# A quarter of the products of E and v summed over two taps on VectorE in chunks 1 to 3, and one normalized tile transposed by DMA instead of TensorE

## The chip, the cores and the metric

The kernel runs on one core of a Trainium2 chip. The metric is the device time of one execution in microseconds (us). A profile of one execution gives the time of every instruction on TensorE (PE, with its weight loads as PEld), VectorE (DVE), ScalarE (ACT), GpSimd (POOL) and of the DMA queue that SyncE (SP) feeds.

## The reference: what is computed

The input x has 2048 rows of 512 numbers. It is normalized row by row, and the result feeds two branches: a local attention with 32 heads of 16 numbers, and a gated network with an inner width of 1792.

```python
xn = _layernorm(x, axis=-1)
s = _A_ref(xn, A_wqkv, A_wo)
g = _silu(_B_ref(xn, B_w_gate, B_w_up, B_w_down))
return x + s * g
```

In the attention every position looks at eight positions of its own head: itself and those 2, 4, ... 14 rows earlier. These eight are called taps here. The logits are products of q and k summed over 16 numbers; after the softmax, the weights of the eight taps multiply v, and the sum over the taps goes through wo:

```python
off = jnp.arange(W) * dil                      # W = 8, dil = 2
logits = jnp.einsum("bhsd,bhswd->bhsw", q, kg) * scale
attn = _softmax(logits, axis=-1)
o = jnp.einsum("bhsw,bhswd->bhsd", attn, vg)
```

The network is `_gelu(xn @ w_gate) * (xn @ w_up)` times w_down, then silu.

## The kernel before, in words

The rows are worked in NJ = 4 chunks of TQ = 512 columns (positions lie along the free dimension, features along the 128 partitions). For a chunk j the program is written out by hand in this order (L618 to L647): 14 `glu` steps (L437), each with four matmuls for the gate and four for the up projection, two ScalarE copies out of PSUM (gelu, and plain) and one VectorE product h; then 12 `qkv` steps of the next chunk (L295), whose PSUM results ScalarE copies to q, k and a staging tile for v; then four `down` steps (L450) of 14 matmuls each; then `divide` and four `finish` steps (L466), which multiply the attention with wo, combine both branches and store. All other work hangs on these steps through a table: `at(("glu", j, 3), ...)` (L487) has a function called just before that step. Each engine runs its instructions in the order in which they are emitted, so this table fixes what stands behind what.

The attention of a chunk goes as follows.

- `qk_products` (L320, VectorE) makes eight tiles q times shifted k. It is called during `qkv` of the same chunk (chunk 0: during `glu`).
- `logits` (L339, TensorE) sums them to eight taps times 32 heads, and ScalarE's exp writes E, with the low two bits of the tap (wl) and the head on the partitions, and the high bit (wh) and the position along the free dimension.
- v goes through DRAM (vT, L288 to L293) and is read back by `load_v` (L300) four times, each time shifted by two more positions, into the four groups of 32 partitions. So v_arr has tap wl and head on the partitions like E, and its 520 columns per feature let wh = 0 and wh = 1 be read as two windows, 8 columns apart.
- `av_product` (L399, VectorE) makes for four of the 16 features (a group g) and one wh the product of E and v in bfloat16: eight tiles per chunk. In chunks 1 to 3 they are called before `glu` steps 3 to 10 (L526, L527). For chunks 2 and 3 each is two instructions of 1024 columns, before that one of 2048.
- `sums(j)` (L508), called after the first `down` step (for the last chunk, before its `glu` step 12), has on TensorE the denominators, then `av_sums` (L412), and then the logits of the next chunk. Besides, it has the reciprocals on VectorE, a trip of these through DRAM (`rs_d`, `rb`), and `load_v` of the next chunk. `av_sums` sums the products over the four wl and both wh: 32 matmuls with 32 output columns each, four of them (i = 0 to 3) to four different groups of 32 PSUM partitions, wh = 0 starting and wh = 1 ending an accumulation.

Rows must also be normalized and transposed (xnT) ahead of their chunk. `moments` (L198) and `normalize` (L208) are VectorE work with one small GpSimd instruction; `transpose_by_dma` (L249) has the DMA write the transposed tile, `transpose` (L235) takes four TensorE transposes into PSUM and a ScalarE copy out of it. Tiles are of 128 rows. Tile 4, the first of chunk 1, is transposed by TensorE ahead of `glu` step 0 of chunk 0 (L609), tile 5 by DMA in two halves, one ahead of `load_v(0)` and one behind it (L610 to L612), tiles 6 and 7 whole by DMA behind that. For chunk 3, the `moments` run before `glu` steps 10 to 13 of chunk 1 and `normalize` before `qkv` steps 0 to 3 of chunk 2 (L498, L499).

Buffers that matter: PSUM tiles of `glu`, `qkv`, `down` and `finish` share four slots (`mm`, L74); ge and u have three slots each (`sm`, L67), h 14 (`hp`), the q tile one (`qp`, 4 KB per partition), the products share 12 (`prod`, L63), v_arr has one, shared with four of the tiles of q times k (tag "va").

Of the kernel before, what the change touches and what calls it, by code (L numbers as in the profile page):

```python
# [8 lines left out]
ALU = mybir.AluOpType  # L9
AF = mybir.ActivationFunctionType  # L10
BF16 = mybir.dt.bfloat16
F32 = mybir.dt.float32

P = 128
# [3 lines left out]
DIL = 2  # L18
WL = 4
WH = 2  # L20
PAD = 16
TQ = 512
# [6 lines left out]
def kernel(  # L29
# [13 lines left out]
    nc = tc.nc  # L43
    B, S, D = A_x.shape
    DF = B_w_gate.shape[1]
    NT, NC, NF, NJ = S // P, D // P, DF // P, S // TQ
    TPQ = TQ // P
# [5 lines left out]
    def pool(name, bufs, **kw):  # L53
        return ctx.enter_context(tc.tile_pool(name=name, bufs=bufs, **kw))
# [4 lines left out]
    qp = pool("qp", 1)  # L59
    kp = pool("kp", 2)  # L60
    ep = pool("ep", 1)
    vap = pool("vap", 1)
    prod = pool("prod", 12)  # L63
    hp = pool("hp", 14)
    xtp = pool("xtp", 2)
    op = pool("op", 1)
# [48 lines left out]
    def load_late_weights():  # L115
# [18 lines left out]
        out=vT.rearrange("(k p) n -> p k n", p=P)[:, :, 0:PAD],  # L134
# [134 lines left out]
    st = [dict(pk={}, pv={}, vst={}) for _ in range(NJ)]  # L269

    def copy_out(j, fo, ps, i0=0, n=TQ, m=1, copy=None):

        which, c = divmod(fo, NC)
        if which == 0:
            if "q" not in st[j]:
                st[j]["q"] = qp.tile([P, NC, TQ], BF16, name="q_sb")
            dst = st[j]["q"][:, c : c + m, i0 : i0 + n]
        elif which == 1:
            dst = k_sb[j][:, c : c + m, PAD + i0 : PAD + i0 + n]
        else:  # L280
            if c // 2 not in st[j]["vst"]:
                st[j]["vst"][c // 2] = vsp.tile([P, 2, TQ], BF16, name="vst")
            dst = st[j]["vst"][c // 2][:, c % 2 : c % 2 + m, i0 : i0 + n]
        if copy is None:
            nc.scalar.activation(out=dst, in_=ps, func=AF.Copy)  # L285
        else:
            copy(out=dst, in_=ps)
        if which == 2 and (c + m) % 2 == 0 and i0 + n == TQ:  # L288
            r, lo = slice((c // 2) * 2 * P, (c // 2 + 1) * 2 * P), PAD + j * TQ
            nc.sync.dma_start(  # L290
                out=vT[r, lo : lo + TQ].rearrange("(c p) n -> p c n", p=P),
                in_=st[j]["vst"][c // 2][:],
            )  # L293

    def qkv(j, fo):  # L295
        ps = mm.tile([P, 1, TQ], F32, name="qkv_ps", tag="mm")
        project(ps[:, 0, :], wqkv_sb, fo * P, j)
        copy_out(j, fo, ps[:])
# [40 lines left out]
    def logits(j):  # L339
        if j == 0:  # L340
            nc.scalar.preload_act_table(AF.Exp)
            quad = att.tile([P, NC, TQ], F32, name="L_ps", tag="quad")
            L = [quad[:, wh, :] for wh in range(WH)]
        else:
            L = [mm.tile([P, TQ], F32, name="L_ps", tag="mm")[:] for _ in range(WH)]
        E = st[j]["E"] = ep.tile([P, WH, TQ], BF16, name="E")
        for wh in range(WH):
            for c in range(NC):
                for wl in range(WL):
                    nc.tensor.matmul(  # L350
                        L[wh][H * wl : H * (wl + 1), :],
                        lhsT=dsum[:, c, :],
                        rhs=st[j]["pk"][WL * wh + wl][:, c, :],
                        start=(c == 0),
                        stop=(c == NC - 1),
                    )
        for wh in range(WH):
            nc.scalar.activation(out=E[:, wh, :], in_=L[wh], func=AF.Exp, scale=SCALE)
        if j == 0:
            for w in range(1, W):  # L360
                wh, wl = divmod(w, WL)
                nc.gpsimd.memset(E[H * wl : H * (wl + 1), wh, 0 : w * DIL], 0.0)

    def denominators(j):

        E = st[j]["E"]
        den = mm.tile([P, P], F32, name="den_ps", tag="mm")
        for wh in range(WH):
            for q in range(4):
                nc.tensor.matmul(  # L370
                    den[H * q : H * (q + 1), :],
                    lhsT=hsum[:],
                    rhs=E[:, wh, q * P : (q + 1) * P],
                    start=(wh == 0),
# [24 lines left out]
    def av_product(j, g, wh):  # L399
# [3 lines left out]
        for d in range(0, 4, n):  # L403
            nc.vector.tensor_tensor(  # L404
                out=pv[:, d : d + n, :],
                in0=st[j]["E"][:, wh, :].unsqueeze(1).to_broadcast([P, n, TQ]),
                in1=st[j]["va"][:, 4 * g + d : 4 * g + d + n, lo : lo + TQ],
                op=ALU.mult,
            )
        st[j]["pv"][g, wh] = pv  # L410

    def av_sums(j):  # L412

        o = att.tile([P, NC, TQ], F32, name="o_ps", tag="quad")
        for g in range(NC):
            for wh in range(WH):
                for i in range(4):
                    nc.tensor.matmul(  # L418
                        o[H * i : H * (i + 1), g, :],
                        lhsT=hsum[:],  # L420
                        rhs=st[j]["pv"][g, wh][:, i, :],
                        start=(wh == 0),
                        stop=(wh == WH - 1),
                    )
        st[j]["o"] = o

# [60 lines left out]
    def at(key, fn, *args):  # L487
        side.setdefault(key, []).append((fn, args))
# [5 lines left out]
    for i in range(TPQ):  # L494
        at(("down", 0, 1), moments, 2 * TPQ + i)
        at(("down", 0, 2), normalize, 2 * TPQ + i)
        at(("glu", 1, 0) if i else ("down", 0, 3), transpose_by_dma, 2 * TPQ + i)
        at(("glu", 1, 10 + i), moments, 3 * TPQ + i)  # L498
        at(("qkv", 2, i), normalize, 3 * TPQ + i)  # L499
        at(("glu", 2, 0) if i else ("down", 1, 3), transpose_by_dma, 3 * TPQ + i)  # L500

    for w in range(W):
        at(("glu", 0, w), qk_products, 0, [w], 0, NC)
    at(("glu", 0, 9), logits, 0)
    for i in range(8):
        at(("glu", 0, 9 + i) if i < 5 else ("qkv", 1, 0), av_product, 0, i // 2, i % 2)

    def sums(j):  # L508

        if j + 1 < NJ:  # L510
            nc.scalar.preload_act_table(AF.Exp)
        denominators(j)
        av_sums(j)
        if j + 1 < NJ:
            logits(j + 1)
        reciprocals(j)
        store_reciprocals(j)
        spread_reciprocals(j)
        if j + 1 < NJ:
            load_v(j + 1)  # L520

    for j in range(1, NJ):
        at(("qkv", j, 2), k_halo, j)
        for i in range(2):
            at(("qkv", j, 4 + 4 * i), qk_products, j, range(W), 2 * i, 2)
        for i in range(8):  # L526
            at(("glu", j, 3 + i), av_product, j, i // 2, i % 2)  # L527
    at(("glu", NJ - 1, 12), sums, NJ - 1)


# [6 lines left out]
    for _, ps in pairs:  # L537
        nc.tensor.matmul(
            ps, lhsT=zero[:], rhs=nc.const_aps.tensor(1.0, [P, 2, HQ], BF16),
            start=True, stop=False,  # L540
# [53 lines left out]
    for fo, ps in pairs:  # L594
        copy_out(0, fo, ps, 0, HQ, 2, nc.vector.tensor_copy if fo >= 8 else None)
# [5 lines left out]
    for n, fo in enumerate((0, 2, 4, 6, 8, 10)):  # L601
        ps = mm.tile([P, 2, HQ], F32, name="qkv_ps", tag="mm")

        w = HQ if n else P
        for i0 in range(0, HQ, w):
            for i in range(2):
                project(ps[:, i, i0 : i0 + w], wqkv_sb, (fo + i) * P, 0, HQ + i0, w)
        copy_out(0, fo, ps[:], HQ, HQ, 2)
    at(("glu", 0, 0), transpose, TPQ)  # L609
    at(("glu", 0, 0), transpose_by_dma, TPQ + 1, (0, 1))  # L610
    at(("glu", 0, 0), load_v, 0)
    at(("glu", 0, 0), transpose_by_dma, TPQ + 1, (2, 3))  # L612
    at(("glu", 0, 0), transpose_by_dma, TPQ + 2)
    at(("glu", 0, 0), transpose_by_dma, TPQ + 3)
    at(("glu", 0, 0), load_late_weights)
    for j in (2, 3):
        at(("glu", 0, 0), load_x, j * TPQ, TPQ)
# [58 lines left out]
```

## Time and profile before

| | us |
|---|---|
| time, median of 3 runs (lowest, highest) | 227.48 (227.48, 227.54) |
| span of the profiled execution | 225.6 |
| busy: TensorE | 220.3 |
| busy: VectorE | 151.9 |
| busy: ScalarE | 131.8 |
| busy: GpSimd | 22.0 |

The busy times show how full each engine is over the whole span. Which of them sets the end is read from the chain of waits: the profile follows the work that ended last backwards, step by step, to what released it. An engine that is not on that chain may be idle or busy without changing the time; how long it could be late is read from the time line of its instructions. One row of a time line is: start, length, engine, line, operation, output and inputs, shapes, count, and in brackets the idle time before it with what ended it.

### The profile page before, as it was taken

Reading aid. Unit: us, or ns where it says so; the run is one execution under the profiler, and the core shown is the slowest. Engines: PE = TensorE matmul, PEld = TensorE weight load, DVE = VectorE, ACT = ScalarE, POOL = GpSimd, SP = SyncE. Lnnn points to the kernel's source line nnn. Section 1 sums busy time; section 2 is a strip of 40 time slices with the busy share of each in tenths; the row PEclk is TensorE's granted clock in tenths of the full one; section 3 lists DMA queues with packets and bytes.
Section 4 is the critical chain, followed back from the end, with each engine's and each line's share of the span. In section 5 each row is a group of like instructions: output and inputs, shape, how many; then the busy total and the mean of one; then the engine's idle time right before and its main releaser. Section 6 shows DMA issues by size and latency. Waiting matters only on the chain.

```text
span 225.6 us, 3579 instructions
## 1 busy us (share of the span) xinstructions
PE 220.3 (98%) x1317; PEld 106.3 (47%) x1338; DVE 151.9 (67%) x281; ACT 131.8 (58%) x208; POOL 22.0 (10%) x67
## 2 busy tenths in 40 slices
PE   8999999999999999999999999999999999999994
PEld 4994444444444444444444444444444444444443
DVE  4688973999974499969804859924934358972352
ACT  4387779676721876767652466676763357655211
POOL 1026971000210000320000000000000000000000
PEclk9999999999999999999999999999999999999999
DMA  6998699952079910000219990000218940001002
GB/s 201 370 402 254 136 198 202 335 175 96 17 160 200 195 23 0 3 1 0 94 32 187 198 180 3 0 0 0 90 25 168 200 116 0 0 0 33 1 23 70
DMA packets 29746, 24.76 MB, mean 110 GB/s; under 512 B 10528, under 2 KB 29216, under 8 KB 29728
## 3 DMA queue, kind: packets, MB, share of 16 engines
q1 hardware_dynamic: 29728, 24.53, 45.1%
q8 instruction: 10, 0.16, 0.3%
q14 instruction: 8, 0.07, 0.1%
HBM read 18.74 MB, written 4.34 MB: 102 GB/s over the span
## 4 chain that ended last, share of the span: by engine, by line
PE 95%; ACT 1%; DVE 1%; DMA 1%; issue 1%; ACTq 0%
PE u_ps L261 22%; PE y_ps L455 21%; PE g_ps L261 20%; PE qkv_ps L261 16%; PE s_ps L471 6%; PE L_ps L350 3%; PE o_ps L418 3%; PE qk_ps L547 2%; ACT u L445 1%; DMA x_sb<-in_A_x_dram 1%; PE v_ps L547 1%; DVE stats L187 1%; PE den_ps L370 0%; PE tr L220 0%; PE trb L220 0%
## 5 line engine op out<-in xcount | busy, mean ns | idle before, releaser
L261 PE MATMUL u_ps<-xnT,wu_sb 128*128 128x512 bf16 x220 | 57.1, 379 | 0.4
L261 PE MATMUL g_ps<-xnT,wg_sb 128*128 128x512 bf16 x218 | 56.5, 379 | 0.2
L455 PE MATMUL y_ps<-wd_sb,h 128*128 128x512 bf16 (+2 forms) x233 | 49.3, 366 | 0.2
L445 ACT ACTIVATE u<-u_ps 128x512 bf16<-128x512 f32 x56 | 33.5, 598 | 16.9 <-PE u_ps L261 16.6
L443 ACT ACTIVATE ge<-g_ps 128x512 bf16<-128x512 f32 x56 | 33.5, 598 | 16.9 <-PE g_ps L261 15.9
L404 DVE TENSOR_TENSOR pv<-E,v_arr 128x1024 bf16<-128x1024 bf16 (+1 forms) x48 | 39.9, 863 | 3.7 <-DMA v_arr<-vT 3.7
L332 DVE TENSOR_TENSOR pk<-q_sb,k_sb 128x1024 bf16<-128x1024 bf16 (+1 forms) x56 | 39.0, 765 | 4.6 <-ACT k_sb L285 4.6
L447 DVE TENSOR_TENSOR h<-ge,u 128x512 bf16<-128x512 bf16 x56 | 23.8, 425 | 23.7 <-ACT u L445 22.1
L261 PE MATMUL qkv_ps<-xnT,wqkv_sb 128*128 128x512 bf16 (+2 forms) x197 | 36.8, 344 | 0.2
L455 PEld LDWEIGHTS <-h 128*128 128x128 bf16 x238 | 22.6, 98 | 26.5 <-issue 1.3
L261 PEld LDWEIGHTS <-wu_sb 128*128 128x128 bf16 x224 | 21.9, 98 | 26.5
L261 PEld LDWEIGHTS <-wg_sb 128*128 128x128 bf16 x224 | 21.7, 98 | 26.6 <-issue 0.8
L463 ACT ACTIVATE sl<-y_ps 128x512 bf16<-128x512 f32 (+2 forms) x17 | 9.7, 572 | 32.4 <-PE y_ps L455 28.9
L261 PEld LDWEIGHTS <-wqkv_sb 128*128 128x128 bf16 x200 | 18.9, 98 | 17.5
L479 DVE TENSOR_TENSOR m<-s_ps,sl 128x512 bf16<-128x512 f32 (+2 forms) x17 | 11.1, 655 | 19.7 <-PE s_ps L471 19.7
L430 DVE TENSOR_TENSOR oT<-o_ps,rb 128x1024 bf16<-128x1024 f32 x8 | 9.4, 1220 | 12.3 <-DMA rb<-rs_d 12.2
L204 POOL TENSOR_TENSOR rstd<-rstd,mhalf 128x1 f32<-128x1 f32 x12 | 8.0, 669 | 71.1 <-DVE rstd L201 71.1
L471 PE MATMUL s_ps<-wo_sb,oT 128*128 128x512 bf16 (+2 forms) x65 | 14.6, 366 | 0.2
L285 ACT ACTIVATE vst<-qkv_ps 128x512 bf16<-128x512 f32 x14 | 8.4, 597 | 3.7 <-PE qkv_ps L261 3.7
L285 ACT ACTIVATE k_sb<-qkv_ps 128x512 bf16<-128x512 f32 x14 | 8.4, 601 | 3.2 <-PE qkv_ps L261 3.2
L285 ACT ACTIVATE q_sb<-qkv_ps 128x512 bf16<-128x512 f32 x14 | 8.3, 603 | 3.0 <-PE qkv_ps L261 3.0
L471 PEld LDWEIGHTS <-oT 128*128 128x128 bf16 x68 | 6.5, 98 | 7.3
(64 smaller groups left out, 128.3 us busy)
## 6 DMA issues: line engine op xcount, KB each, us to landing
v_arr<-vT SPq DMA_DIRECT2D x16, 520.0 KB, 8.3
vT<-vst SPq DMA_DIRECT2D x8, 256.0 KB, 2.2
out_dram<-o_t SPq DMA_DIRECT2D x15, 128.0 KB, 3.4
wg_sb<-in_B_w_gate_dram SPq DMA_DIRECT2D x2, 896.0 KB, 10.2
wu_sb<-in_B_w_up_dram SPq DMA_DIRECT2D x2, 896.0 KB, 12.1
wd_sb<-in_B_w_down_dram SPq DMA_DIRECT2D x1, 1792.0 KB, 11.8
wqkv_sb<-in_A_wqkv_dram SPq DMA_DIRECT2D x4, 384.0 KB, 4.6
x_sb<-in_A_x_dram SPq DMA_DIRECT2D x3, 512.0 KB, 7.7
```

What stands on the lines that cost most here:

```text
L261: nc.tensor.matmul(ps, lhsT=w[:, dk, lo : lo + P], rhs=xnT[j][:, dk, i0 : i0 + n], start=(dk == 0), stop=(dk == NC - 1),)
L285: nc.scalar.activation(out=dst, in_=ps, func=AF.Copy)
L332: nc.vector.tensor_tensor(out=st[j]["pk"][w][:, c0 : c0 + n, :], in0=st[j]["q"][:, c0 : c0 + n, :], in1=k_sb[j][:, c0 : c0 + n, off : off ...
L404: nc.vector.tensor_tensor(out=pv[:, d : d + n, :], in0=st[j]["E"][:, wh, :].unsqueeze(1).to_broadcast([P, n, TQ]), in1=st[j]["va"][:, 4 * ...
L430: nc.vector.tensor_tensor(out=oT[:, g : g + 2, :], in0=st[j]["o"][:, g : g + 2, :], in1=st[j]["rb"][:].unsqueeze(1).to_broadcast([P, 2, TQ ...
L443: nc.scalar.activation(out=ge[:], in_=g_ps[:], func=AF.Gelu_apprx_tanh)
L445: nc.scalar.activation(out=u[:], in_=u_ps[:], func=AF.Copy)
L447: nc.vector.tensor_tensor(out=h[:], in0=ge[:], in1=u[:], op=ALU.mult)
L455: nc.tensor.matmul(y[:], lhsT=st[j][fc][:, tt * P : (tt + 1) * P], rhs=wd_sb[:, fc, cols], start=(fc == 0), stop=(fc == NF - 1),)
L463: nc.scalar.activation(out=sl[:], in_=y[:], func=AF.Silu)
L471: nc.tensor.matmul(s[:], lhsT=st[j]["oT"][:, g, tt * P : (tt + 1) * P], rhs=wo_sb[:, g, cols], start=(g == 0), stop=(g == NC - 1),)
L479: nc.vector.tensor_tensor(out=m[:], in0=s[:], in1=sl[:], op=ALU.mult)
```

## The change

There are three edits.

1. For group g = 0 (four of the 16 features) in chunks 1 to 3, a new function `av_pair` takes the place of two calls of `av_product`. For each of the four features it multiplies both halves of E with the two windows of v in one instruction, into a float32 tile `two` of 2 x 512 columns, and adds the two halves in a second instruction to one bfloat16 tile. The sum over wh is thus done by VectorE, and `av_sums` needs one pass of four matmuls for this group instead of two. The tile `two` takes the slot of q, whose last reader of that chunk is done by then. E is stored with wh reversed (`Eb`), so that its first half belongs to the window at column 0. The products of the other groups move from before `glu` steps 3 to 10 to before steps 1, 3, 5, 7, 9 and 10, and the pairs stand before steps 2, 4, 6 and 8.
2. `moments` and `normalize` of chunk 3 move from `glu` of chunk 1 and `qkv` of chunk 2 to the `down` steps of chunk 1, which leaves room on VectorE in `glu` of chunk 1.
3. Tile 4 is transposed by DMA, ahead of `load_v(0)`. Tile 5 is transposed whole behind it, and no half goes ahead.

Its aim is to take instructions from TensorE and give their work to VectorE and to the DMA.

```diff
-        E = st[j]["E"] = ep.tile([P, WH, TQ], BF16, name="E")
+        Eb = st[j]["Eb"] = ep.tile([P, WH, TQ], BF16, name="E")
+        E = st[j]["E"] = Eb[:, ::-1, :]
...
+    def av_pair(j, g, d):
+        if d == 0:
+            st[j]["pv"][g] = prod.tile([P, 4, TQ], BF16, name="pv", tag="prod")
+            st[j]["two"] = qp.tile([P, WH, TQ], F32, name="two", tag="q")
+        two = st[j]["two"]
+        v = st[j]["va"][:, 4 * g + d, 0:TQ]
+        nc.vector.tensor_tensor(
+            out=two[:],
+            in0=st[j]["Eb"][:],
+            in1=bass.AP(
+                tensor=v.tensor, offset=v.offset, ap=[v.ap[0], [WL * DIL, WH], [1, TQ]]
+            ),
+            op=ALU.mult,
+        )
+        nc.vector.tensor_tensor(
+            out=st[j]["pv"][g][:, d, :], in0=two[:, 0, :], in1=two[:, 1, :], op=ALU.add
+        )
...
         for g in range(NC):
-            for wh in range(WH):
+            pv = st[j]["pv"]
+            pvs = [pv[g]] if g in pv else [pv[g, wh] for wh in range(WH)]
+            for n, p in enumerate(pvs):
                 for i in range(4):
                     nc.tensor.matmul(
                         o[H * i : H * (i + 1), g, :],
                         lhsT=hsum[:],
-                        rhs=st[j]["pv"][g, wh][:, i, :],
-                        start=(wh == 0),
-                        stop=(wh == WH - 1),
+                        rhs=p[:, i, :],
+                        start=(n == 0),
+                        stop=(n == len(pvs) - 1),
                     )
...
-        at(("glu", 1, 10 + i), moments, 3 * TPQ + i)
-        at(("qkv", 2, i), normalize, 3 * TPQ + i)
+        at(("down", 1, 1), moments, 3 * TPQ + i)
+        at(("down", 1, 2), normalize, 3 * TPQ + i)
...
-        for i in range(8):
-            at(("glu", j, 3 + i), av_product, j, i // 2, i % 2)
+        for i in range(6):
+            at(("glu", j, 1 + i + min(i, 4)), av_product, j, 1 + i // 2, i % 2)
+        for d in range(4):
+            at(("glu", j, 2 + 2 * d), av_pair, j, 0, d)
...
-    at(("glu", 0, 0), transpose, TPQ)
-    at(("glu", 0, 0), transpose_by_dma, TPQ + 1, (0, 1))
+    at(("glu", 0, 0), transpose_by_dma, TPQ)
     at(("glu", 0, 0), load_v, 0)
-    at(("glu", 0, 0), transpose_by_dma, TPQ + 1, (2, 3))
-    at(("glu", 0, 0), transpose_by_dma, TPQ + 2)
-    at(("glu", 0, 0), transpose_by_dma, TPQ + 3)
+    for t in range(TPQ + 1, 2 * TPQ):
+        at(("glu", 0, 0), transpose_by_dma, t)
```

More of the change, by code (lines that the diff above doesn't have):

```diff
@@ L275, in copy_out @@
             if "q" not in st[j]:
-                st[j]["q"] = qp.tile([P, NC, TQ], BF16, name="q_sb")
+                st[j]["q"] = qp.tile([P, NC, TQ], BF16, name="q_sb", tag="q")
             dst = st[j]["q"][:, c : c + m, i0 : i0 + n]
```

## The prediction, made before the result was known

> **What bounds the kernel now.** I read the page's busy shares, then the chain of work that ended last in order of time, then VectorE's time line, and last the DMA share by stretches. The page:
>
> ```profile
> PE 220.3 (98%) x1317; PEld 106.3 (47%) x1338; DVE 151.9 (67%) x281; ACT 131.8 (58%) x208; POOL 22.0 (10%) x67
> ...
> PE 95%; ACT 1%; DVE 1%; DMA 1%; issue 1%; ACTq 0%
> ```
>
> TensorE carries the whole chain. The rest is the first load ahead of it and the last store. The chain in order of time (start, length, what):
>
> ```profile
> 11.67 5.27 PE qkv_ps L261 x56
> 16.94 0.22 PE tr L220 x4
> 17.17 0.21 PE g_ps L261
> ...
> 110.75 1.73 PE o_ps L418 x32
> ...
> 164.61 1.73 PE o_ps L418 x32
> ...
> 201.63 1.73 PE o_ps L418 x32
> 203.36 0.97 PE g_ps L261 x4
> ```
>
> The pieces join without a gap: the four transposes of tile 4 (L220) and the sums over the taps (L418) are on the path with their full length. Where the chain passes through ScalarE (0.61 us at 81.70, for one) TensorE isn't idle: from 80.74 to 83.33 three groups of 0.86 us fit exactly. So each matmul taken away shortens the end by what it streams, as long as no other engine becomes late. VectorE in chunk 3, before:
>
> ```profile
> 183.14 0.43 DVE L447 TENSOR_TENSOR h<-ge,u 128x512 bf16<-128x512 bf16 x1 [0.60 <-ACT u L445]
> 184.87 0.43 DVE L447 TENSOR_TENSOR h<-ge,u 128x512 bf16<-128x512 bf16 x1 [1.30 <-ACT u L445]
> 186.59 0.42 DVE L447 TENSOR_TENSOR h<-ge,u 128x512 bf16<-128x512 bf16 x1 [1.30 <-ACT u L445]
> 186.94 1.28 DVE L404 TENSOR_TENSOR pv<-E,v_arr 128x1024 bf16<-128x1024 bf16 x2
> 188.32 0.43 DVE L447 TENSOR_TENSOR h<-ge,u 128x512 bf16<-128x512 bf16 x1
> ...
> 199.02 1.29 DVE L404 TENSOR_TENSOR pv<-E,v_arr 128x1024 bf16<-128x1024 bf16 x2
> 200.41 0.43 DVE L447 TENSOR_TENSOR h<-ge,u 128x512 bf16<-128x512 bf16 x1
> ```
>
> h comes every 1.73 us, TensorE's step of eight matmuls; a pair of products just fills the time between. More VectorE work here makes h late. Prices, by shape:
>
> ```profile
> L404 DVE TENSOR_TENSOR pv<-E,v_arr 128x1024 bf16<-128x1024 bf16 x32 | 20.6, 685 | 0.0
> L404 DVE TENSOR_TENSOR pv<-E,v_arr 128x2048 bf16<-128x2048 bf16 x16 | 19.3, 1220 | 3.7 <-DMA v_arr<-vT 3.7
> L479 DVE TENSOR_TENSOR m<-s_ps,sl 128x512 bf16<-128x512 f32 x15 | 10.3, 686 | 18.3 <-PE s_ps L471 18.3
> L430 DVE TENSOR_TENSOR oT<-o_ps,rb 128x1024 bf16<-128x1024 f32 x8 | 9.4, 1220 | 12.3 <-DMA rb<-rs_d 12.2
> ```
>
> [...] 1024 elements cost 685 or 1220 ns.
>
> [...] The trace before has a float32 input (1220 ns) but no float32 product output. [...] 32 matmuls in 1.73 us is 0.054 each, while matmuls of full width take 0.86/4 = 0.216. [...]
>
> **The change part by part.**
>
> TensorE. Per chunk 1 to 3 four of 32 matmuls of `av_sums` go, one full set of four column groups: 4 x 0.054 = 0.216 us, in three chunks 0.65. The transposes of tile 4: 0.22. ScalarE's copy of that tile goes too (0.59 at 17.47), off the path. Weight loads go with their matmuls. Sum: 0.87 us.
>
> VectorE. A pair is one product with 2 x 512 float32 out and one sum of 512 from float32. I take the rows with a float32 operand: 1.22 and 0.69. Issued one behind another, independent instructions start sooner than their length says: 16 products of 1024 took 9.72 us, 0.61 each for 0.69; one of 2048 follows another instruction by 1.14 (37.52 to 38.66); h by 0.34. A dependent one starts 0.03 behind the end (m 178.21 + 0.69, o_t 178.93). So a pair takes 1.25 + 0.61 = 1.86. Two steps of `glu` now hold two h, one product (1.21, or 1.14 in chunk 1) and one pair: 0.68 + 1.21 + 1.86 = 3.75 against TensorE's 3.45. VectorE falls behind by 0.3 per pair, over four pairs 1.2.
>
> Walking chunk 3 in the clock of before: h(0) 183.14, product, h(1) 184.87, pair to 187.07, where h(2) was due at 186.59 (late 0.5); late by 0.8 at h(4), 1.1 at h(6), 1.4 at h(8), 1.0 at h(10); then it catches up 1.38 a step. The last product ends at 201.5 instead of 200.3. Its readers are the last four matmuls of `av_sums`, due at 201.63 + 24 x 0.054 = 202.93, and both clocks are shifted alike: 1.4 us in hand.
>
> In chunk 1 the walk gives at most 1.8 late. In chunk 2 products now begin behind h(0), about 129.2 - 0.4 us, but `load_v(2)`, last issued at about 119.6 and landing 11.3 later, lands near 130.9, less the 0.2 by which its release moves: VectorE waits some 1.5 us with h(1) behind it, and the walk gives at most 2.7 late. Chunk 1's v_arr lands at about 76.0, its first product is due 76.4; chunk 3's at 182.2, due 182.8, both about in time.
>
> How late may h be? h's queue holds ge and u. In chunk 1 ge of a step starts 1.55 ahead of its h (80.78, 82.33) and needs the h three steps back to have ended: 3 x 1.73 - 1.55 - 0.43 = 3.2 us late before ScalarE waits. Its PSUM slot is wanted by TensorE two steps on, 1.95 later than it is free now: 5.1 us before TensorE waits. 2.7 is well inside, so the VectorE work is costed at nothing.
>
> Moved `moments` and `normalize`: 4 x 1.01 + 1.38 = 5.4 us behind the reciprocals of chunk 1 (end 111.9), done by 117.3. VectorE waited there for rb until 119.05 (7.16 us), and the transpose of tile 12 is issued at 120.3. Nothing.
>
> The q slot: `two` needs q's readers done, VectorE itself; the next q copy by ScalarE waits for the last sum, some 5 us ahead. Nothing.
>
> DMA. Ahead of `load_v(0)` stands now a whole tile instead of a half (18.05). DMA shares (last but one column) by stretch:
>
> ```profile
> 21.00:22.00 1.00, 1.00 (x7) 0.42 (x5) 1.00 (x1) 0.73 (x2) 0.65 (x7) 1.00 0.27 50
> 22.00:23.00 1.00, 1.00 (x6) 0.46 (x5) 1.00 (x3) 0.71 (x2) 0.81 (x5) 1.00 0.04 12
> 23.00:24.00 1.00, 1.00 (x6) 0.47 (x5) 1.00 (x3) 0.60 (x1) 1.00 (x1) 1.00 0.00 0
> ```
>
> `load_v(0)` starts at 23.07, held by the landing of vT at 22.2, and the engines idle ahead of it. Three whole tiles at 75.23 to 79 took about 3.0 us of full share, so the extra half is some 0.5 us and fits. If not: v_arr(0) at 37.5 opens a VectorE stretch without a pause to 58.0, the last product of q and k. The logits read it at 58.62 - 0.22 + 27 x 0.054 = 59.86, 1.86 in hand. The half that moves behind `load_v(0)` delays xnT of chunk 1 by about 0.5: it landed by 29.7 + 8.9 = 38.6, wanted at 43.07. The weights for `glu` step 0 (5.59 + 11.0 = 16.6) are there in time too.
>
> **Unknown costs.** The float32 product: [...] I take 1.22. The extra half tile: 0.5 us by the share, at most half of its issue to landing, 5.4/2 = 2.7. The DMA round trip of the reciprocals of chunk 1 took 3.4 us (111.92 to 115.33), in others 1.5; twice the excess would bring 4.6 late, still inside 5.1.
>
> **The rivals.**
> - The float32 product runs at half rate. [...] Against it: the rows with float32 inputs[...]. 6%.
> - The whole tile ahead of `load_v(0)` costs 2.3 to 2.7 us there, and the logits of chunk 1 wait 0.4 to 0.8: 227.1, no change. Against it: the idle stretch above. 6%.
> - Waits that I costed at nothing take up part: h late beyond 3.2 in chunk 2 with small stalls of 0.2 to 0.3 us, or a bubble at a shorter set of sums: 226.85, still faster. 10%.
>
> **How the numbers follow.** 227.48 - 0.87 = 226.61. The likeliest case, 78%, ends within 0.2 of it. The range takes in the partial loss and the edge of the second rival, 226.35 to 227.1, and leaves out the first. Faster (below 227.03) 0.87, the same 0.06, slower 0.07.
>
> **What would show it.** Right: L418 with 116 matmuls, 1.51 us in chunks 1 to 3; no L220 piece at 16.9; `two` near 1.22 us; h at most 1.9 late in chunks 1 and 3 and 2.7 in chunk 2; TensorE's chain without gaps. Wrong: [...] a wait of the sums for pv near 201, ScalarE's ge waiting for h, or logits waiting for pk near 59.

## The result, and the profile after

The changed kernel takes 226.81 us (median of 6 runs, 226.36 to 227.06) against 227.48 us (median of 6 runs, 227.32 to 227.54). The ratio is 0.9969, 95% interval 0.9956 to 0.9982: 0.3% faster. The prediction was 226.6, within 226.35 to 227.1. The saving in the medians is 0.67 us, where 0.87 had been worked out; the section after the experiments takes up the missing 0.2 us.

From the page of the changed kernel, the engines' busy times and the shares of the chain that ended last:

```profile
PE 219.9 (98%) x1301; PEld 106.4 (47%) x1322; DVE 164.4 (73%) x295; ACT 131.4 (58%) x207; POOL 22.0 (10%) x67
...
PE 96%; ACT 1%; issue 1%; DVE 0%; ACTq 0%
```

VectorE has 12.5 us more work, TensorE 16 matmuls less, and the chain is still TensorE's. From the same chain in order of time (start, length, what):

```profile
12.02 5.27 PE qkv_ps L261 x56
17.29 0.22 PE g_ps L261
...
110.88 1.51 PE o_ps L442 x28
...
164.52 1.51 PE o_ps L442 x28
...
201.33 1.51 PE o_ps L442 x28
202.84 0.97 PE g_ps L261 x4
```

The four transposes that stood between the last qkv matmul and the first gate matmul are gone (16.94 to 17.17 before). The sums over the taps (now L442) have 28 matmuls in 1.51 us where there were 32 in 1.73, and the gate matmuls join them without a gap at 202.84. But the first line starts at 12.02 us, where before it started at 11.67, and nothing in the program ahead of it has changed.

From VectorE's time line in `glu` of chunk 3, its start and the rows around the last product, which stand in the order in which the program emits them (start, length, engine, line, operation, output and inputs, shapes, count, idle time before it):

```profile
182.84 0.42 DVE L471 TENSOR_TENSOR h<-ge,u 128x512 bf16<-128x512 bf16 x1 [0.60 <-ACT u L469]
183.18 1.28 DVE L406 TENSOR_TENSOR pv<-E,v_arr 128x1024 bf16<-128x1024 bf16 x2
184.56 0.42 DVE L471 TENSOR_TENSOR h<-ge,u 128x512 bf16<-128x512 bf16 x1
184.91 1.22 DVE L422 TENSOR_TENSOR two<-E,v_arr 128x1024 f32<-128x1024 bf16 x1
186.16 0.69 DVE L430 TENSOR_TENSOR pv<-two 128x512 bf16<-128x512 f32 x1
...
199.84 1.28 DVE L406 TENSOR_TENSOR pv<-E,v_arr 128x1024 bf16<-128x1024 bf16 x2
201.05 0.41 DVE L471 TENSOR_TENSOR h<-ge,u 128x512 bf16<-128x512 bf16 x1
```

VectorE has no idle time from 183.18 to the last product, but what it does is in time: the last product ends at 201.12 (199.84 + 1.28), while its readers, the last four matmuls of the sums, are due at 201.33 + 24 x 0.054 = 202.63. The prices of the two new instructions, from the groups by shape:

```profile
L422 DVE TENSOR_TENSOR two<-E,v_arr 128x1024 f32<-128x1024 bf16 x12 | 14.6, 1216 | 0.0
L430 DVE TENSOR_TENSOR pv<-two 128x512 bf16<-128x512 f32 x12 | 8.3, 692 | 0.4
```

### The profile page after: what moved, and what is told of

It is laid out like the page before. It is cut to its first block, busy times and chain, and to the rows that moved or that the text cites. A ratio compares the mean times of both kernels' runs of the same rounds, so it can differ in the third digit from the quotient of the medians.

```text
span 225.1 us, 3562 instructions
## 1 busy us (share of the span) xinstructions
PE 219.9 (98%) x1301; PEld 106.4 (47%) x1322; DVE 164.4 (73%) x295; ACT 131.4 (58%) x207; POOL 22.0 (10%) x67
## 4 chain that ended last, share of the span: by engine, by line
PE 96%; ACT 1%; issue 1%; DVE 0%; ACTq 0%
PE u_ps L261 22%; PE y_ps L479 21%; PE g_ps L261 20%; PE qkv_ps L261 16%; PE s_ps L495 6%; PE L_ps L352 3%; PE o_ps L442 3%; PE qk_ps L574 2%; ACT u L469 1%; PE v_ps L574 1%; PE warm_ps L244 1%; PE qk_ps L565 1%; PE den_ps L372 0%; PE v_ps L565 0%; PE trb L220 0%
## 5 line engine op out<-in xcount | busy, mean ns | idle before, releaser
L406 DVE TENSOR_TENSOR pv<-E,v_arr 128x1024 bf16<-128x1024 bf16 (+1 forms) x38 | 32.3, 880 | 1.9 <-ACT E L360 1.9
L204 POOL TENSOR_TENSOR rstd<-rstd,mhalf 128x1 f32<-128x1 f32 x12 | 7.0, 582 | 90.1 <-DVE rstd L201 90.1
L454 DVE TENSOR_TENSOR oT<-o_ps,rb 128x1024 bf16<-128x1024 f32 x8 | 9.4, 1219 | 7.7 <-PE y_ps L479 6.0
L422 DVE TENSOR_TENSOR two<-E,v_arr 128x1024 f32<-128x1024 bf16 x12 | 14.6, 1216 | 0.0
```

The source lines that it names most:

```text
L406: nc.vector.tensor_tensor(out=pv[:, d : d + n, :], in0=st[j]["E"][:, wh, :].unsqueeze(1).to_broadcast([P, n, TQ]), in1=st[j]["va"][:, 4 * ...
L422: nc.vector.tensor_tensor(out=two[:], in0=st[j]["Eb"][:], in1=bass.AP(tensor=v.tensor, offset=v.offset, ap=[v.ap[0], [WL * DIL, WH], [1, T ...
```

## The experiments

For every kernel I also read from the chain how long the program runs from the start of the 56 qkv matmuls, behind all that was seen to vary in the first 12 us, to the start of the last sum on VectorE. I call this the body. Starts and bodies are from one profile each. Each ratio compares with runs of the kernel before that stood beside that kernel; their medians lie between 227.48 and 227.54.

| kernel | time, median us | ratio to before (95%) | start of body | body |
|---|---|---|---|---|
| before | 227.48 | | 11.67 | 211.28 |
| the changed kernel | 226.81 | 0.9969 (0.9956 to 0.9982) | 12.02 | 210.41 |
| e1_tile4 | 227.25 | 0.9986 (0.9975 to 0.9997) | 11.82 | 211.06 |
| e2_pairs | 226.82 | 0.9969 (0.9956 to 0.9981) | 11.72 | 210.64 |
| e3_again | 226.68 | 0.9962 (0.9949 to 0.9974) | 11.89 | 210.41 |
| e6_two_tiles | 226.66 | 0.9961 (0.9948 to 0.9975) | 11.84 | 210.41 |
| e4_twice12 | 230.24 | 1.0117 (1.0102 to 1.0132) | 11.87 | 214.12 |
| e5_twice3 | 230.77 | 1.0138 (1.0123 to 1.0153) | 11.73 | 214.20 |
| e7_bf16_all | 224.74 | 0.9878 (0.9864 to 0.9893) | 12.26 | 208.46 |
| e9_bf16_all_again | 224.63 | 0.9871 (0.9854 to 0.9889) | 11.84 | 208.47 |
| e8_bf16_c0 | 224.99 | 0.9893 (0.9876 to 0.9909) | 12.12 | 208.25 |
| e10_bf16_c0_again | 224.76 | 0.9881 (0.9863 to 0.9900) | 11.62 | 208.38 |

### Each part alone, and the whole once more

The transposes alone (on the kernel before):

```diff
-    at(("glu", 0, 0), transpose, TPQ)
-    at(("glu", 0, 0), transpose_by_dma, TPQ + 1, (0, 1))
+    at(("glu", 0, 0), transpose_by_dma, TPQ)
     at(("glu", 0, 0), load_v, 0)
-    at(("glu", 0, 0), transpose_by_dma, TPQ + 1, (2, 3))
-    at(("glu", 0, 0), transpose_by_dma, TPQ + 2)
-    at(("glu", 0, 0), transpose_by_dma, TPQ + 3)
+    for t in range(TPQ + 1, 2 * TPQ):
+        at(("glu", 0, 0), transpose_by_dma, t)
```

> The kernel before with the third edit alone: tile 4 transposed whole by DMA ahead of the load of v for chunk 0, tile 5 whole behind it. Theory (each matmul taken from TensorE shortens the end by what it streams): 0.22 us less, 227.26, and from the start of the 56 qkv matmuls to the end of the span 0.22 less than before. Rival (the parts pay less than they stream, and the missing 0.2 us of the whole change is lost in one of them): less than 0.1 us here, if it is this part. If only the time ahead of the first transposes differs, the rival has no ground.

The pairs are the changed kernel with this edit taken back. That leaves edits 1 and 2 together; edit 2, the moved normalization, was not run by itself:

> The changed kernel with the transposes of tiles 4 and 5 as before (edits 1 and 2 alone). Theory: 0.65 us less than before, 226.83; o_ps 1.51 us in chunks 1 to 3. Rival: the pairs pay only some 0.45, because VectorE is late somewhere; then TensorE must show a gap in a glu stage or ahead of the sums.

And the changed kernel without any edit:

> The changed kernel once more, unaltered, to see how its time and its first 6 us vary. Theory: the sum of the two parts, 0.87 us, whenever the first transposed tile starts at 4.9 us as in the profile of before; up to 0.35 less[...], so 226.4 to 227.0. Rival: the saving is 0.67 us in every run, with the start at 4.9 as well.

The bodies are 0.22 us (211.28 to 211.06) and 0.64 us (to 210.64) shorter for the parts, and 0.87 us (to 210.41) for the whole, in both profiles of it. The parts add up to a hundredth. No part pays less than it streams, so the rival theory falls. The medians, 0.26, 0.69 and 0.83 us below the 227.51 of the runs of before that stood beside them, say the same more roughly. One part of my expectation for the third run was wrong: it started its first transposed tile at 4.83 us, as early as the kernel before, and yet its body started at 11.89. So the speed of TensorE's first matmuls isn't all that moves the start; more on that below.

### Two tiles ahead of the load of v

```diff
     at(("glu", 0, 0), transpose_by_dma, TPQ)
+    at(("glu", 0, 0), transpose_by_dma, TPQ + 1)
     at(("glu", 0, 0), load_v, 0)
-    for t in range(TPQ + 1, 2 * TPQ):
+    for t in range(TPQ + 2, 2 * TPQ):
         at(("glu", 0, 0), transpose_by_dma, t)
```

> The changed kernel with tile 5 also transposed ahead of the load of v for chunk 0, so that two whole tiles stand ahead of it instead of one. Theory (1.9 us in hand at the logits of chunk 1): v lands 0.5 to 1.5 us later than in the changed kernel, VectorE starts its products later by as much, and the time is the same within 0.1 us. Rival (a tile ahead of the load costs 2.3 us or more): the logits of chunk 1 wait near 59 us and the time grows by 0.4 us or more.

The time is the same (226.66 us) and the body too. v is there at 37.82 us, where the profiles with one tile ahead have 37.43 (e3_again) and 37.91 (e1_tile4), and before, with half a tile, 37.52. The second tile thus delays v by less than these differ (0.48 us), not by the 0.5 to 1.5 us that I expected. That fits the idle time of the DMA engines: in the changed kernel, with one whole tile ahead, the stretches (PE, PEld, DVE, ACT, POOL busy, granted clock, DMA share, GB/s) still have the hole, two microseconds at a share of 0.05:

```profile
22.00:24.00 2.00, 2.00 (x11) 0.88 (x9) 2.00 (x4) 1.44 (x3) 1.69 (x7) 1.00 0.05 8
```

The rival of a dear transfer ahead of the load falls.

### How much later VectorE may be: the slack by itself

The slack is how late VectorE may be before TensorE waits. To find it, the float32 product of each pair is issued twice, in chunks 1 and 2, or in chunk 3 alone (with `j == 3` for `j < 3`):

```diff
-        nc.vector.tensor_tensor(
-            out=two[:],
...
+        for _ in range(2 if j < 3 else 1):
+            nc.vector.tensor_tensor(
+                out=two[:],
...
```

> The changed kernel with the float32 product of each pair issued twice in chunks 1 and 2 (the same output twice, so the result is the same), 1.14 us more VectorE work per pair. Theory (TensorE waits once h is 5.1 us late): h(8) is late by 1.8 + 4.6 = 6.3 us in chunk 1 and 1.3 + 4.6 = 5.9 in chunk 2 if nothing waits; TensorE waits 1.2 and 0.8 us, so 2.0 us slower than the changed kernel, 228.8. Rival 1 (the slack is only the 3.2 us after which ScalarE waits): 3.1 + 2.7 = 5.8 us slower, 232.6. Rival 2 (VectorE in glu isn't tied to TensorE at all): no change.

> The changed kernel with the float32 product of each pair issued twice in chunk 3 alone. Theory: the last product of E and v ends at 201.1 + 4.6 = 205.7 us, TensorE's last four matmuls of the sums want it at 202.6, so TensorE waits 3.1 us there (part of it perhaps earlier, in glu) and the time is 229.9. Rival (the deadline at the sums isn't binding, only h is): 0.8 us slower, 227.6.

With more work in chunks 1 and 2 the body is 3.71 us longer than the changed kernel's (214.12 against 210.41). That lies between my 2.0 and the 5.8 of rival 1; rival 2, no change, falls. The time lines of that kernel in chunk 1, ScalarE's and then TensorE's, show where the loss is:

```profile
86.68 0.60 ACT L468 ACTIVATE ge<-g_ps 128x512 bf16<-128x512 f32 x1 [0.95 <-DVE h L472]
...
91.61 0.60 ACT L468 ACTIVATE ge<-g_ps 128x512 bf16<-128x512 f32 x1 [2.37 <-DVE h L472]
```

```profile
92.25 1.02 PE L261 MATMUL g_ps<-xnT,wg_sb 128*128 128x512 bf16 x4 [0.31 <-ACT ge L468]
...
97.18 1.02 PE L261 MATMUL g_ps<-xnT,wg_sb 128*128 128x512 bf16 x4 [1.32 <-ACT ge L468]
```

ScalarE's ge waits for h, and the gate matmuls wait for ge: the mechanism is the one that the prediction named. ScalarE waits first at 86.68, for an h(4) that is 3.9 us late (86.17 against 82.30), and TensorE loses nothing by it; so rival 1 falls as well. TensorE's first wait comes at 92.25. From 72.95 (first gate matmul) to 99.07 (first qkv matmul) this kernel takes 26.12 us, the changed kernel 24.17 (73.10 to 97.27): 1.95 us lost in chunk 1, and 1.76 in chunk 2.

Both sizes of the expectation were off. First, the second product, with the same output as the first, starts 0.02 us behind its end, so one more costs 1.27 us (78.11 to 80.63 for both and the dependence, against 1.25 for one), not 1.14. Second, the threshold for TensorE comes out of its two waits. h(6), behind the third pair, is 5.33 us late (91.09 against 85.76), and TensorE loses 0.47; h(8) is 6.81 late (96.02 against 89.21), less the 0.47 already lost, and TensorE loses 1.48. Both give 4.86 us, where the prediction had 5.1. The same two waits in chunk 2 give 4.85 and 4.83. About half of the difference lies in hand-overs between engines that the prediction left out: in the chain of this kernel 0.08 us pass from the end of h to ge (96.45 to 96.53) and 0.04 from ge to the gate matmuls (97.14 to 97.18). With 1.27 and 4.86 the expectation would have been 1.8 + 5.1 - 4.86 = 2.0 in chunk 1 (1.95 measured) and 1.3 + 5.1 - 4.86 = 1.5 in chunk 2 (1.76; there v landed only at 131.67, and VectorE waited 0.35 us for it).

In chunk 3 the loss is 3.79 us (214.20), where I expected 3.1; the rival with 0.8 falls. TensorE's time line of that kernel:

```profile
202.86 1.33 PE L443 MATMUL o_ps<-pv,hsum 128*32 128x512 bf16 x19 [1.61 <-DVE pv L431]
...
205.34 0.39 PE L443 MATMUL o_ps<-pv,hsum 128*32 128x512 bf16 x2 [0.54 <-DVE pv L406]
205.94 0.39 PE L443 MATMUL o_ps<-pv,hsum 128*32 128x512 bf16 x2 [0.21 <-DVE pv L406]
```

First the sums wait for the last pair, whose group is first in their order, and then for each later product. TensorE has no wait ahead of the sums here, so in chunk 3 their deadline is the tighter one. Four times 1.27 in place of 1.14 explains 0.5 of the 0.7 us. The rest is the end of the sums: the last two matmuls start behind the last product and take 0.39 us (205.94 to 206.33), where I had counted 0.054 each, as in an unbroken row. In the changed kernel the next gate matmuls start 1.72 us behind the last product (201.12 to 202.84), here 0.44 (205.89 to 206.33). So the slack at the sums is 1.3 us, and not the 1.5 between the last product and its due time.

### More from the same idea: bfloat16, two features at once, all groups

The experiments say that TensorE's saving comes in full as long as VectorE keeps within its slack. The float32 tile costs VectorE 1.86 us per feature (184.91 to the next h at 186.77). If the two products of a pair stay in bfloat16, as they did before the change, two features should fit in the same time: before, 2048 products in bfloat16 took 1220 ns and 1024 took 685. The sum of the two is rounded to bfloat16 as in the changed kernel. So all four groups of chunks 1 to 3 can be summed on VectorE:

```diff
-            st[j]["two"] = qp.tile([P, WH, TQ], F32, name="two", tag="q")
+        if "two" not in st[j]:
+            st[j]["two"] = qp.tile([P, 2, WH, TQ], BF16, name="two", tag="q")
...
-            in0=st[j]["Eb"][:],
+            in0=st[j]["Eb"][:].unsqueeze(1).to_broadcast([P, 2, WH, TQ]),
             in1=bass.AP(
-                tensor=v.tensor, offset=v.offset, ap=[v.ap[0], [WL * DIL, WH], [1, TQ]]
+                tensor=v.tensor, offset=v.offset,
+                ap=[v.ap[0], [VW, 2], [WL * DIL, WH], [1, TQ]],
...
-            out=st[j]["pv"][g][:, d, :], in0=two[:, 0, :], in1=two[:, 1, :], op=ALU.add
+            out=st[j]["pv"][g][:, d : d + 2, :],
+            in0=two[:, :, 0, :], in1=two[:, :, 1, :], op=ALU.add,
...
+        for i, fc in enumerate((1, 2, 3, 5, 6, 7, 9, 10)):
+            at(("glu", j, fc), av_pair, j, i // 2, 2 * (i % 2))
```

> All four groups of chunks 1 to 3 in pairs, with the products kept in bfloat16 and two features per instruction: a product of 2 x 2 x 512 and a sum of 2 x 512, eight of each per chunk. VectorE: 1.25 + 0.61 = 1.86 us for two features, 14.9 per chunk, about as much as the changed kernel's 14.7. Theory: TensorE loses 16 of 32 matmuls of the sums in three chunks, 3 x 0.86 = 2.59, and the transposes, 0.22: 224.67, and h is late by no more than 1.5 us. [...]

It takes 224.74 us, ratio 0.9878 (0.9864 to 0.9893), and once more 224.63, 0.9871 (0.9854 to 0.9889): faster than both kernels. In its trace h is late by up to 2.3 us in chunk 1 (90.21 against 87.87) and 2.0 in chunk 2, where I had expected no more than 1.5, and TensorE waits for it nowhere. The body is 2.82 us shorter than before, where 12 x 4 matmuls and the transposes give 2.81. From its groups by shape and its chain:

```profile
L422 DVE TENSOR_TENSOR two<-E,v_arr 128x2048 bf16<-128x2048 bf16 x24 | 29.3, 1219 | 0.5 <-DMA v_arr<-vT 0.5
...
L431 DVE TENSOR_TENSOR pv<-two 128x1024 bf16<-128x1024 bf16 x24 | 16.6, 692 | 0.8
```

```profile
111.11 0.86 PE o_ps L444 x16
```

2048 products in bfloat16 take as long as 1024 into float32 (1219 and 1216 ns), and 1024 bfloat16 sums as long as 512 of float32 (692 both). Before, without the overlapping windows of v, 2048 products in bfloat16 took 1220 ns, so the windows cost nothing that shows.

Last, the first group of chunk 0 in pairs too:

```diff
     for i in range(8):
-        at(("glu", 0, 9 + i) if i < 5 else ("qkv", 1, 0), av_product, 0, i // 2, i % 2)
+        if i < 2:
+            at(("glu", 0, 9 + i), av_pair, 0, 0, 2 * i)
+        else:
+            at(("glu", 0, 9 + i) if i < 5 else ("qkv", 1, 0), av_product, 0, i // 2, i % 2)
```

> As the kernel with all groups of chunks 1 to 3 in bfloat16 pairs, and also the first group of chunk 0. Theory: four matmuls less, 0.22 us, 224.45; VectorE has 1.4 us more work between the landing of v and the logits of chunk 1, whose last products of q and k end by 59.0 to 59.5 against a due time of about 60.0. Rival (the slack there is smaller): the logits of chunk 1 wait, and the gain is lost, 224.7 or more.

Both kernels were run side by side once more:

> The kernel with all groups of chunks 1 to 3 in bfloat16 pairs once more, beside the one that also has the first group of chunk 0 in pairs. Theory: 224.4 to 225.1, and 208.46 us from the start of the 56 qkv matmuls to the start of the last sum, as in its first profile; whatever differs lies in the first 12 us.

> The kernel that also has the first group of chunk 0 in pairs once more. Theory: 0.21 us less from the start of the 56 qkv matmuls to the start of the last sum (208.25), and the median 0.2 us under the other's, if the first 12 us fall alike. Rival: it is slower in time as its first four runs were (224.99 against 224.74), so something in chunk 0 waits in most runs, and its profile shows a gap of TensorE near 40 or 59 us.

The first profile has the 0.21 us in the body (208.25), the second only 0.09 (208.38). In its chain the logits of chunk 1 take longer than the 1.73 us that they stream:

```profile
58.13 1.86 PE L_ps L352 x32
```

Their last operand is there at 59.34 (49.63 + 9.71), 0.25 us ahead of 27 x 0.054 behind the start, and yet they lost 0.13 us. So the slack at this place ends some 0.4 us ahead of what that sum would say, as at the sums of chunk 3. In time the step shows no gain, so both expectations of 0.2 us were missed: 224.99 and 224.76 us against 224.74 and 224.63. Its medians are higher both times, by less than the 0.57 and 0.66 us over which its own runs spread, so whether chunk 0 gains or loses stays open; by these runs it is not worth having.

## Why the prediction was right, point by point

- **TensorE's sum.** Right to the hundredth. L418 (now L442) has 116 matmuls, 1.51 us in chunks 1 to 3; the piece of L220 at 16.9 is gone; the body is 0.87 us shorter, 0.22 for the transposes and 0.64 for the pairs, each also alone.
- **From the sum to the time.** Here 0.2 us are missing: the prediction took the start for granted, and the start varies. In the profile of before TensorE waits at 4.92 us for VectorE's xn. In that of the changed kernel it then still has its own first matmuls to finish. The same four matmuls with a zero weight, and the first four v matmuls behind them, in the kernel before and in the changed kernel, and the zero matmuls in the changed kernel once more:

```profile
2.92 1.69 PE L538 MATMUL qk_ps<-const-bfloat16-1.0,zero 128*128 128x512 bf16 x4
...
5.52 0.38 PE L547 MATMUL v_ps<-xnT,wqkv_sb 128*128 128x128 bf16 x4
```

```profile
2.92 1.91 PE L565 MATMUL qk_ps<-const-bfloat16-1.0,zero 128*128 128x512 bf16 x4
...
5.73 0.57 PE L574 MATMUL v_ps<-xnT,wqkv_sb 128*128 128x128 bf16 x4
```

```profile
2.92 1.50 PE L565 MATMUL qk_ps<-const-bfloat16-1.0,zero 128*128 128x512 bf16 x4
```

  The zero matmuls start at the same time and take 1.50 to 1.91 us with the same instructions (1.36 in e10_bf16_c0_again). In the changed kernel's profile the matmuls behind them are slow for longer too, and by 6.2 us the 0.35 us by which its body starts later (12.02 against 11.67) have come together. But the zero matmuls alone don't set the start: in the seven profiles where they take 1.91 us the body starts anywhere from 11.72 to 12.26. The arrival of the third tile of x can hold it too: in e8_bf16_c0 the chain runs through a transfer of x that ends at 8.56 us (3.14 + 5.42), then through VectorE to the transposes at 10.84, which stand at 10.53 in the kernel before. VectorE first used that tile at 7.58 us in the changed kernel's profile, at 8.14 in that of before, at 8.36 in e3_again and at 8.58 in e8_bf16_c0, and against before the last two start their body later by the same 0.22 and by 0.45 us (11.89 and 12.12).

  Over twelve profiles the body starts between 11.62 and 12.26, over kernels that are the same up to there, and repeated runs of the kernel before spread from 227.18 to 228.63. For the two profiled executions the later start is all that is missing: their spans differ by 0.5 us (225.6 and 225.1), which is the 0.87 of the bodies less 0.35. That the 0.2 us in the medians have the same cause fits this, and the 0.83 of the changed kernel's second set of runs, but it isn't shown for executions without a profile. Why TensorE's first matmuls speed up earlier in one run than in another isn't shown either: the granted clock reads 1.00 in both profiles from the first microsecond. The stated range held the result partly by luck: its upper part had been drawn for waits on other engines, and none of those came.
- **VectorE's prices.** That a float32 output costs what a float32 input does (1220 ns for 1024 elements before) was my estimate, since no product before had a float32 output. Right: 1216 and 692 ns against 1.22 and 0.69, the sum 1.25 us behind the product (184.91, 186.16). The walk gave h(8) 1.4 us late in chunk 3 and 1.8 in chunk 1; the profile has 1.3 (197.97 against 182.84 + 8 x 1.727) and 1.8 (91.13 against 89.36). The last product ends at 201.12, 1.5 us ahead of its readers' due time; 1.4 was predicted, of which by e5_twice3 some 0.2 can't be used. The rival of a float32 product at half rate, which would be 2 x 1.22 = 2.4 us by the same row, falls.
- **Chunk 2.** The walk gave 2.7 us late, because v would land late. In the profile of the changed kernel v was in time and h(8) 1.3 late: the trip of the reciprocals through DRAM took 1.5 us (112.01 to 113.47), as in ten of the twelve profiles, where before it took 3.4, and so `load_v(2)` was issued at 116.20. But in e2_pairs, with the same VectorE work, the trip took 3.2 us (111.93 to 115.16), and VectorE did wait for v:

```profile
130.78 1.29 DVE L406 TENSOR_TENSOR pv<-E,v_arr 128x1024 bf16<-128x1024 bf16 x2 [1.24 <-DMA v_arr<-vT]
```

  There h(8) was 2.5 us late (145.39 against 129.12 + 8 x 1.727), neither ScalarE nor TensorE waited for it, and the body is shorter by the full 0.64. So the case that the prediction reckoned with does occur, and it lies inside the slack. Why the trip takes 1.5 us in most runs and over 3 in two isn't shown.
- **How late h may be.** ScalarE's wait and then TensorE's came in the predicted order (e4_twice12); the threshold for TensorE is 4.9 us, 5.1 was predicted. In all kernels without a doubled product h stayed within 3.1 us.
- **DMA.** Right that it fits, and cheaper than put: the extra half tile was costed at 0.5 us, and none of it can be seen. With half a tile ahead of the load v is there at 37.4 and 37.5 us, with one tile at 37.4 to 37.9 (in the profile of the changed kernel by 35.9, where VectorE waited for E instead), with two at 37.8. Of the 1.86 us in hand at the logits of chunk 1 some 0.4 can't be used, by e10_bf16_c0_again. That what is issued ahead of `load_v(0)` is also moved ahead of it was my assumption; no run shows it.
- **Moved normalization.** The last normalized tile of chunk 3 ended at 117.25 (115.87 + 1.38), 117.3 was predicted, and `divide` started at 117.91. The body shows no loss by it.

## What to carry to other kernels

In this kernel TensorE carries the chain without gaps. What was taken from it was worth what it streams (0.22 us for the four transposes, 0.64 for twelve matmuls of 32 columns, 0.054 each beside three others), and the work that replaced it on VectorE was free up to a slack that can be worked out from slots and due times: 4.9 us for h, 1.3 us at the sums. A deadline that is reckoned from an unbroken row of matmuls came out too late by 0.2 us at the sums and 0.4 at the logits; at the sums the two matmuls behind the late operand took 0.39 us, not 2 x 0.054. Work out the slack before choosing how much to move. With float32, a second group would add an estimated 4 x 1.86 - 2 x 1.21 = 5.0 us of VectorE work per chunk, about what e4_twice12 and e5_twice3 added, which cost 1.8 to 3.8 us in each of these chunks; with bfloat16 and two features an instruction there was room for all groups. When the expected gain is as small as the variation of the first microseconds, compare the part of the trace behind it.

## What the runs showed of the hardware

- The same four first matmuls (128x512), issued at the same time, took from 1.36 to 1.91 us in twelve executions, and what followed started up to 0.6 us apart (11.62 to 12.26). I had not expected a run to differ there by so much.
- 28 matmuls of 32 columns in a row, in sets of four to four groups of PSUM partitions, took 1.51 us, 0.054 each; two that started behind a wait took 0.39 us together.
- Two VectorE products with the same output didn't overlap: the second started 0.02 us behind the end of the first, and both took 2.48 us. Sixteen products of 1024 elements with different outputs took 9.72 us, 0.61 each, for a length of 0.69.
- A product of bfloat16 inputs with a float32 output took 1216 ns for 1024 elements; with a bfloat16 output, E read twice and overlapping windows of v, 2048 took 1219 ns.
